# The last head of a decode kernel: an earlier signal for a value buffer, a split load, a new order of chunks and a fifth weight buffer

## Chip, cores, metric

One NeuronCore of a Trainium2 chip. The metric is device time in microseconds from the first to the last instruction as the runs report it; the profile's span is 1.8 us shorter (1923.6 against 1925.44 in the profiled run of the kernel before). Lower is better.

## The reference

One token (Sq = 1) goes through pre-LN attention over a cache and a dense block:

```
D = 640; H, Sk, Dh = 32, 32768, 192; Dff = 1536        # bf16 inputs
q = (layernorm(x) @ wq), split into 32 heads
p = softmax(q . k_cache * Dh**-0.5);   o = p @ v_cache
h  = x + concat(o) @ wo
out = h + relu(layernorm(h) @ w1) @ w2
```

The work is reading: 805 MB of keys and values and 20 MB of weights, each used once.

## The kernel before

Each head's 32768 keys are cut into chunks. For a chunk, VectorE computes the scores of some keys itself (multiply by q, sum), TensorE those of the rest (transposes **T**, then products **S**; ScalarE copies the transposes out of PSUM in between). ScalarE turns scores into weights by exp, into buffers pA (VectorE's keys) and pB (TensorE's). TensorE then sums the values by these weights (**V**). T4, S4, V4 below are those of chunk 4 of the last head; V(30,7) is the sum of chunk 7 of head 30. SyncE issues all large loads, in program order, and waits before each for its place to be free; GpSimd passes most landings on to TensorE (POOLq in the traces). In the code, the label `("PV", h, c)` says that V(h,c) is done, `den_mm` adds up the weights of a head, `o_turn` turns a head's result for the projection. A value tile ("first, second, third values" of the last head) holds two chunks' values; the two places `vt[0]`, `vt[1]` alternate. The last head reads its final quarter in small pieces (the "end keys" and "end values") so that little is left to do after the last byte.

```python
def vals(h, ld):                       # SyncE: one value tile
    if ld == 1 and h > 0:
        g.wait("PV", h, 0)             # V(h,0) done: says that V(h-1,7), before it, has left vt[1]
    elif ld > 1:
        g.wait("PV", h, 2 * ld - 3)
    elif h > 0:
        g.wait("PV", h - 1, 5)
    ...
    load(vt[ld % NV][:], src, f"dv{ld % NV}", "v", h, ld)

# SyncE, last head (LAST = 31):
for ld in range(NL - 1):               # NL = 4
    ...                                # key tile ld
    vals(LAST - 1, NL - 1) if ld == 0 else vals(LAST, ld - 1)   # written as if/else in the kernel
for i, jl in enumerate(ENDJ):          # three end-key loads, no wait of their own
    end_keys(NL - 1 + i, k0, jl, f"dke{1 + i}")
vals(LAST, NL - 2)                     # third values, waits for V1
...                                    # end values (wait for V1), w1 (waits for V3), w2 in three pieces

def pe_end(g):                         # TensorE, last head
    transposes(g, h, 0); den_mm(g, h - 1); scores_pe(g, h, 0)
    for c in range(1, NC - 2):         # c = 1..5
        transposes(g, h, c)
        values(g, *((h - 1, NC - 3 + c) if c < 3 else (h, c - 3)))
        scores_pe(g, h, c)
        if c == 3: o_turn(g, h - 1)
    transposes(g, h, 6); values(g, h, 3)
    for c in (7, 8, 9):
        transposes(g, h, c)
        if c > 7: values(g, h, c - 4)  # V4 before S7, V5 before S8
        scores_pe(g, h, c - 1)
    values(g, h, 6); scores_pe(g, h, 9); values(g, h, 7)
    den_mm(g, h); values(g, h, 8); values(g, h, 9)
    ...                                # projection, norm, both dense layers, output
```

Statements are joined on a line here to save room. The projection of every head pair is added up in PSUM, in the bank `attT`, over the whole run: one starting matmul at the very beginning, all later ones of the projection with `start=False`.

The softmax here doesn't subtract the row's maximum and nothing guards it: scores larger than these inputs give would overflow.

## Time and profile before

| | before |
|---|---|
| median of 3 runs (lowest, highest) | 1924.14 us (1923.79, 1927.06) |
| profiled run, its span | 1925.44, 1923.6 us |
| DMA busy share in 40 slices | 9 tenths or more in 39 |
| HBM read | 825 MB at 429 GB/s |
| TensorE, VectorE busy | 81%, 81% |

TensorE and VectorE are each busy for four fifths of the time and still neither sets it: the transfers do, until the last head. There the order of loads, their landings and TensorE's waits decide. The prediction below shows the lines.

### The profile page before, as it was taken

Reading aid. Unit: us, or ns where it says so; the run is one execution under the profiler, and the core shown is the slowest. Engines: PE = TensorE matmul, PEld = TensorE weight load, DVE = VectorE, ACT = ScalarE, POOL = GpSimd, SP = SyncE. Lnnn points to the kernel's source line nnn. Section 1 sums busy time; section 2 is a strip of 40 time slices with the busy share of each in tenths; the row PEclk is TensorE's granted clock in tenths of the full one; section 3 lists DMA queues with packets and bytes.
Section 4 is the critical chain, followed back from the end, with each engine's and each line's share of the span. In section 5 each row is a group of like instructions: output and inputs, shape, how many; then the busy total and the mean of one; then the engine's idle time right before and its main releaser. Section 6 shows DMA issues by size and latency. Waiting matters only on the chain.

```text
span 1923.6 us, 36300 instructions
## 1 busy us (share of the span) xinstructions
PE 1554.4 (81%) x15899; PEld 1088.3 (57%) x15899; DVE 1560.5 (81%) x734; ACT 966.9 (50%) x2031; POOL 0.7 (0%) x6
## 2 busy tenths in 40 slices
PE   4878878777888788787777878878878788787897
PEld 3555555555555565555555655655656556555564
DVE  5878888878888798787787878978879788888885
ACT  3544545544555454454454545544545445544553
POOL 0000000000000000000000000000000000000000
PEclk8989898887888887888888888888788798898888
DMA  9999999999999999999999999999999999999997
GB/s 408 433 428 434 435 430 440 429 430 435 429 435 437 426 436 432 432 437 429 438 430 429 438 429 433 439 428 433 431 433 435 430 433 436 431 437 432 430 410 328
DMA packets 35864, 825.25 MB, mean 429 GB/s; under 512 B 3588, under 2 KB 5124, under 8 KB 11140
## 3 DMA queue, kind: packets, MB, share of 16 engines
q1 hardware_dynamic: 35834, 824.98, 99.6%
q8 instruction: 12, 0.20, 0.0%
q14 instruction: 8, 0.07, 0.0%
q10 hardware_dynamic: 10, 0.00, 0.0%
HBM read 824.97 MB, written 0.00 MB: 429 GB/s over the span
## 4 chain that ended last, share of the span: by engine, by line
DMA 55%; PE 35%; ACT 6%; DVE 3%; SPq 1%; issue 0%; POOLq 0%; DVEq 0%
DMA kt<-in_A_k_cache_dram 54%; PE o_ps L368 19%; PE tp L387 10%; ACT kT L587 6%; PE sp L368 4%; PE mm L368 2%; DVE pr L672 1%; DVE sc L675 1%; DMA vt<-in_A_v_cache_dram 1%; PE attT L368 1%; SPq L227 1%; ACT pA L602 0%; POOLq L350 0%; DVE o_pair L686 0%; ACT row_e L607 0%
## 5 line engine op out<-in xcount | busy, mean ns | idle before, releaser
L672 DVE TENSOR_TENSOR pr<-kt,qb 128x2304 f32<-128x2304 bf16 (+2 forms) x257 | 755.9, 2941 | 303.9 <-POOLq L321 278.7
L587 ACT COPY kT<-tp 128x1024 bf16<-128x1024 bf16 (+1 forms) x899 | 817.3, 989 | 321.3 <-PE tp L387 320.4
L387 PE MATMUL tp<-ident_f,kt 128*128 128x128 f32 x3459 | 578.1, 334 | 240.8 <-POOLq L350 238.6
L675 DVE TENSOR_REDUCE sc<-pr 128x12 f32<-128x2304 f32 (+2 forms) x257 | 755.3, 2939 | 8.9
L387 PEld LDWEIGHTS tp<-ident_f,kt 128*128 128x128 f32 x3459 | 501.8, 174 | 252.4 <-POOLq L350 244.0
L368 PE MATMUL o_ps<-vt,pB 128*2 128x384 bf16 x2286 | 459.2, 351 | 7.9 <-POOLq L350 7.1
L593 ACT ACTIVATE pB<-sp 128x20 bf16<-128x20 f32 (+2 forms) x258 | 47.8, 185 | 571.5 <-PE sp L368 571.5
L368 PE MATMUL o_ps<-vt,pA 128*2 128x384 bf16 x1778 | 330.6, 326 | 0.0
L368 PEld LDWEIGHTS o_ps<-vt,pB 128*2 128x2 bf16 x2286 | 187.6, 88 | 233.5 <-issue 92.2
L368 PE MATMUL sp<-qm,kT 128*128 128x2 bf16 x6918 | 214.5, 164 | 106.6 <-ACT kT L587 106.3
L368 PEld LDWEIGHTS sp<-qm,kT 128*128 128x128 bf16 x6918 | 192.5, 98 | 187.6 <-ACT kT L587 144.8
L368 PEld LDWEIGHTS o_ps<-vt,pA 128*2 128x2 bf16 x1778 | 150.0, 84 | 142.0 <-issue 3.5
L602 ACT ACTIVATE pA<-sc 128x12 bf16<-128x12 f32 (+2 forms) x257 | 53.4, 208 | 41.4 <-DVEq L65 40.5
L593 ACT ACTIVATION_READ_ACCUMULATOR pB<-sp 128x1 f32 x258 | 50.2, 194 | 0.0
L602 ACT ACTIVATION_READ_ACCUMULATOR pA<-sc 128x1 f32 x257 | 48.7, 190 | 0.0
L686 DVE TENSOR_SCALAR o_pair<-o_ps,rec 2x384 bf16<-2x384 f32 x32 | 19.4, 605 | 6.3 <-PE o_ps L368 1.7
L368 PE MATMUL mm<-wq_s,xn_ln 128*1 (+1 forms) x160 | 18.7, 248 | 3.7 <-POOLq L350 3.7
L680 DVE TENSOR_REDUCE rec<-mm 128x1 f32<-128x20 f32 x32 | 5.7, 179 | 16.3 <-PE mm L368 11.8
L368 PE MATMUL attT<-oT,wo_s 128*128 128x1 bf16 x465 | 16.4, 164 | 0.3 <-DVE oT L696 0.3
L368 PEld LDWEIGHTS mm<-dsums,ones_mat 128*128 128x128 f32 x64 | 15.1, 291 | 0.3 <-issue 0.3
L368 PEld LDWEIGHTS attT<-oT,wo_s 128*128 128x128 bf16 x465 | 14.5, 101 | 0.4 <-DVE oT L696 0.4
L368 PE MATMUL mm<-ones_row,row_e 1*128 1x1 bf16 x384 | 14.0, 159 | 0.0
(71 smaller groups left out, 145.4 us busy)
## 6 DMA issues: line engine op xcount, KB each, us to landing
vt<-in_A_v_cache_dram SPq DMA_DIRECT2D x127, 3072.0 KB, 18.8
kt<-in_A_k_cache_dram SPq DMA_DIRECT2D x62, 6144.0 KB, 32.4
kt<-in_A_k_cache_dram SPq DMA_DIRECT2D x3, 3072.0 KB, 18.3
wq_s<-in_A_wq_dram SPq DMA_DIRECT2D x4, 1920.0 KB, 22.5
wo_s<-in_A_wo_dram SPq DMA_DIRECT2D x16, 480.0 KB, 9.5
kt<-in_A_k_cache_dram SPq DMA_DIRECT2D x1, 1920.0 KB, 15.4
kt<-in_A_v_cache_dram SPq DMA_DIRECT2D x2, 960.0 KB, 22.4
kt<-in_B_w_dram SPq DMA_DIRECT2D x1, 1920.0 KB, 16.7
```

Source lines behind the costliest of these rows:

```text
L227: g.do(lambda: nc.sync.dma_start(out=dst, in_=src), sem, label, by=16)
L368: return lambda: pe.matmul(o, lhsT=w, rhs=r, **kw)
L387: calls.append(lambda b=b, o=o: pe.transpose(out=dst[:, b, :], in_=src[:, o:o + 2 * P].bitcast(f32), identity=ident_f[:]))
L587: g.do(lambda: act.copy(out=kT[c % 2][:, b0:b0 + nb, :], in_=src[:, 0:nb, :].bitcast(bf16)), "act_pe", ("cp", h, c, k))
L593: g.do(lambda: act.activation(out=pB[c % 4][:, 0:jp], in_=sp[:, 0:jp], func=F.Exp, scale=SCALE, accum_out=dsums[:, 2 * c + 1:2 * c + 2]), ...
L602: g.do(lambda: act.activation(out=pA[c % 4][:, 0:jd], in_=sc[c % NC][:, 0:jd], func=F.Exp, scale=SCALE, accum_out=dsums[:, 2 * c:2 * c + 1 ...
L672: g.chain(lambda: dve.tensor_tensor(out=pr[:, 0:j1 - j0, :], in0=src[:, (off + j0) * Dh:(off + j1) * Dh].rearrange("p (j d) -> p j d", d=D ...
L675: g.chain(lambda: dve.reduce_sum(out=sc[c % NC][:, j0:j1], in_=pr[:, 0:j1 - j0, :], axis=X), "dve")
L680: g.chain(lambda: dve.reduce_sum(out=rec[:, 0:1], in_=mm[:, 0:2 * NCM], axis=X), "dve")
L686: g.do(lambda: dve.tensor_scalar_mul(out=o_pair[:, :, 1, :], in0=o_ps[0:2, 0:2 * Dh].rearrange("q (i d) -> q i d", i=2), scalar1=rec[0:2, ...
```

## The change

Intent: let the last head's second values be issued when their place is free and not one sum later; let TensorE start on the third values when half of them are there, and give it other work until then. The diff's core (the lines of pA/pB that only replace 4 by NB, and the new semaphore's name, are cut):

```diff
+    NB = 5                                    # buffers of pA and pB, were 4
@@ SyncE: vals
-            if ld == 1 and h > 0:
+            if ld == 1 and h == LAST:
+                g.wait("vfree")
+            elif ld == 1 and h > 0:
@@ SyncE: third values in two loads
-        vals(LAST, NL - 2)
+        g.wait("PV", LAST, 1)
+        src = rows(v_hd, LAST, P * JL * (NL - 2), JL)
+        n = J * Dh
+        load(vt[0][:, 0:n], src[:, 0:n], "dv0", "v", LAST, NL - 2)
+        load(vt[0][:, n:2 * n], src[:, n:2 * n], "dvh", "vh")
@@ TensorE: values
+        if h == LAST and c == 5:
+            g.wait("vh")
@@ TensorE: pe_end
             transposes(g, h, c)
-            values(g, *((h - 1, NC - 3 + c) if c < 3 else (h, c - 3)))
+            if c == 1:
+                values(g, h - 1, NC - 2)
+            elif c > 2:
+                values(g, h, c - 3)
             scores_pe(g, h, c)
+            if c == 1:
+                values(g, h - 1, NC - 1)
+                pe_group(g, [mmul(attT[0:1, 500:501], ones_row[0:1, 0:1], zero5[0:1, 0:1], start=True, stop=True,
+                                  skip_group_check=True)], ("vfree",))
@@
-        for c in (7, 8, 9):
-            transposes(g, h, c)
-            if c > 7:
-                values(g, h, c - 4)
-            scores_pe(g, h, c - 1)
-        values(g, h, 6)
-        scores_pe(g, h, 9)
-        values(g, h, 7)
+        transposes(g, h, 7)
+        scores_pe(g, h, 6)
+        transposes(g, h, 8)
+        scores_pe(g, h, 7)
+        transposes(g, h, 9)
+        values(g, h, 4)
+        scores_pe(g, h, 8)
+        scores_pe(g, h, 9)
+        for c in (5, 6, 7):
+            values(g, h, c)
```

The tiny matmul exists because the last sum of each of heads 0 to 30 (chunk 7) signals on a semaphore that the engine loops count down, which SyncE's straight-line program can't wait on; the matmul signals on one that it can.

More of the change, by code (lines that the diff above doesn't have):

```diff
@@ L165 @@
     sc = [sbuf(f"sc{i}", [P, J], f32) for i in range(NC)]
-    pA = [sbuf(f"pA{i}", [P, J], bf16) for i in range(4)]
-    pB = [sbuf(f"pB{i}", [P, J], bf16) for i in range(4)]
+    pA = [sbuf(f"pA{i}", [P, J], bf16) for i in range(NB)]
+    pB = [sbuf(f"pB{i}", [P, J], bf16) for i in range(NB)]
     x_row = sbuf("x_row", [DT, P], bf16)
@@ L217 @@
     names += [f"dk{i}" for i in range(NK)] + [f"dv{i}" for i in range(NV)] + ["dwq", "dwo", "dx", "dout"]
-    names += [f"dke{i}" for i in range(4)] + [f"dve{i}" for i in range(4)] + ["dw1"] + [f"dw2_{i}" for i in range(3)]
+    names += [f"dke{i}" for i in range(4)] + ["dvh"] + [f"dve{i}" for i in range(4)] + ["dw1"] + [f"dw2_{i}" for i in range(3)]
     sems = {n: nc.alloc_semaphore(n) for n in names}
@@ L434, in values @@
         src = v_tile(h, ld)
-        a, b = pA[c % 4], pB[c % 4]
+        a, b = pA[c % NB], pB[c % NB]
         calls = []
@@ L592, in exp_pe @@
         g.wait("S", h, c)
-        g.do(lambda: act.activation(out=pB[c % 4][:, 0:jp], in_=sp[:, 0:jp], func=F.Exp, scale=SCALE,
+        g.do(lambda: act.activation(out=pB[c % NB][:, 0:jp], in_=sp[:, 0:jp], func=F.Exp, scale=SCALE,
                                     accum_out=dsums[:, 2 * c + 1:2 * c + 2]), "act_pe", ("ep", h, c))
@@ L601, in exp_dve @@
         g.wait("sc", h, c)
-        g.do(lambda: act.activation(out=pA[c % 4][:, 0:jd], in_=sc[c % NC][:, 0:jd], func=F.Exp, scale=SCALE,
+        g.do(lambda: act.activation(out=pA[c % NB][:, 0:jd], in_=sc[c % NC][:, 0:jd], func=F.Exp, scale=SCALE,
                                     accum_out=dsums[:, 2 * c:2 * c + 1]), "act_pe", ("ed", h, c))
```

## The prediction

> **What bounds the kernel now.** I read the page first, then the chain of waits over the whole run, then everything after 1845 us in finer views, since the diff acts only there (the five-deep p buffers run in every head, but each head's loop body keeps its order).
>
> The page says that transfers bound the run as a whole: slices of the DMA row are nearly all 9, and the chain is mostly key loads.
>
> ```profile
> GB/s 408 433 428 434 435 430 440 429 430 435 429 435 437 426 436 432 432 437 429 438 430 429 438 429 433 439 428 433 431 433 435 430 433 436 431 437 432 430 410 328
> DMA 55%; PE 35%; ACT 6%; DVE 3%; SPq 1%; issue 0%; POOLq 0%; DVEq 0%
> ```
>
> About 430 GB/s in every slice until the last two (410 and 328). So heads 0 to 30 can't gain from this change; what can gain is the last head, from where the queue starves. The two-microsecond windows (columns: stretch, length, busy of PE, PEld, DVE, ACT, POOL; then granted clock, DMA share, GB/s) show where:
>
> ```profile
> 1869.00:1871.00 2.00, 2.00 (x9) 0.88 (x8) 1.98 (x1) 1.08 (x2) 0.00 (x0) 0.65 0.90 377
> 1871.00:1873.00 2.00, 2.00 (x38) 1.32 (x35) 1.98 (x1) 0.14 (x2) 0.00 (x0) 1.00 0.29 123
> 1873.00:1875.00 2.00, 1.29 (x14) 1.22 (x12) 1.74 (x4) 0.68 (x5) 0.00 (x0) 1.00 1.19 344
> ```
>
> One hole. Against 430 GB/s it loses 2 us x (53 + 307 + 86)/430 = **2.07 us** of transfer time. SyncE's own timeline names its cause:
>
> ```profile
> 1848.12 0.43 SPq L227 DMA_DIRECT2D kt<-in_A_k_cache_dram  x1
> 1872.17 0.33 SPq L227 DMA_DIRECT2D vt<-in_A_v_cache_dram  x1
> 1872.54 1.72 SPq L227 DMA_DIRECT2D kt<-in_A_k_cache_dram  x3
> 1878.36 0.33 SPq L227 DMA_DIRECT2D vt<-in_A_v_cache_dram  x1
> ```
>
> Nothing is issued between 1848.12 and 1872.17, when the queue has run dry. The load at 1872.17 is the last head's second values ("v1"). It waits for the first sum of the last head (V0), and the three end-key loads stand behind it. But its place was read last by the two sums before V0, those of head 30's chunks 6 and 7. On TensorE (start, length, what):
>
> ```profile
> 1861.60 1.46 PE L368 MATMUL o_ps<-vt,pB 128*2 128x384 bf16 x8
> 1862.90 1.46 PE L368 MATMUL o_ps<-vt,pA 128*2 128x384 bf16 x8
> ...
> 1868.41 2.75 PE L368 MATMUL o_ps<-vt,pB 128*2 128x384 bf16 x10
> 1871.00 1.14 PE L368 MATMUL o_ps<-vt,pA 128*2 128x384 bf16 x6
> ```
>
> The place is free at 1864.36; V0 ends at 1872.14. So 7.8 us of the wait guards nothing.
>
> The chain of waits over the end then shows what sets the time:
>
> ```profile
> 1848.12 25.57 DMA kt<-in_A_k_cache_dram
> ...
> 1875.63 2.70 PE o_ps L368 x16
> 1878.34 0.02 issue
> 1878.36 19.60 DMA vt<-in_A_v_cache_dram
> ...
> 1898.05 4.26 PE o_ps L368 x16
> ```
>
> The third values ("v2") are issued when V1 ends and land only at 1897.96, behind v1 and the end keys. Then TensorE works without a real pause to the last sum at 1912.84 (14.8 us), and 10.8 us of projection, norm, dense layers and output follow. So two things matter at the end: when v2 lands, and how much TensorE work is left then. TensorE's idle before V2, T6 and V4 is 2.03, 1.99 and 2.53 us, and its granted clock falls to 0.50 at 1899 to 1901 after the last.
>
> **What the Trainium skill says.** "DMA: Bandwidth & Descriptors", section "Queues, rings and completion order": one issuing engine's queue consumes descriptors in ring order on each DMA engine. The trace agrees: v1, end keys and v2 land in issue order at 1882.5, 1887.9 to 1890.7 and 1898.0. So a load issued early still lands in turn, and only the hole is won on the transfer side. "TensorE: Matmul & The Clock Gate", section "What's actually happening": after an idle window of about 3.4 us TensorE runs at half rate. Here 1.19 to 2.53 us of idle already brought 0.5 in the windows, so this trace is harsher; ten sums then took 3.29 us instead of 1.79. "PSUM — Partial Sum Buffer", section "The four PSUM rules": a starting matmul clears the written-bits of its whole bank in its quadrant. The new signalling matmul has start=True in the bank that holds the projection's running sum; that costs no time, but may concern the values. No record of before can show it.
>
> **The change, part by part.** T, S, V are a chunk's transposes, scores, sums. From this timeline at full clock: T of 15 is 1.85, of 12 1.5, of 9 1.15, of 6 0.8 us; S of 30/24/18/12 is 0.85/0.7/0.5/0.4; V of 16/10/8/4 is 2.7/1.95/1.3/0.65.
>
> *Signal.* V(30,7) moves ahead of T2: S1 ends at 1859.83, V(30,7) at 1862.55, one tiny matmul (0.2 us) tells SyncE, v1 is issued near 1862.9 instead of 1872.17. The end keys follow at once. The hole closes: every later transfer lands 2.07 us earlier. Cost: T2 (now 1862.75) has no sums after it, so S2 waits for ScalarE's four copies (3.5 us from 1863.45) until 1867.05, against 1865.55. After it T3 and V0 at low clock as before (about 5.9 us) end at 1873.7; S3, o_turn, T4 start at 1874.8 instead of 1873.78; V1 ends at 1879.4 and v2 is issued 1 us later than before. That is off the path: the queue then holds v1 and end keys until about 1871 + 14.6 = 1885.6 (6.3 MB at 430).
>
> *Landings after.* v1 1880.4; end keys from 1885.9; v2 whole 1895.9, its first half (3.65 us of bytes less) 1892.2; the four end-value pieces 1898.1 to 1903.2; the last dense weights 1915.0 - 2.07 = 1912.9.
>
> *TensorE after T6* (starts at the key landing, 1885.9; S5 is over at 1885.1): T6 1.15, V3 2.7, T7 1.15, S6 0.55, T8 0.8, wait for T7's copies and chunk 6's exp 0.85, S7 0.5, T9 0.8, V4 2.7, S8 0.4, wait for the exp 0.3, S9 0.4, V5 2.7, V6 and V7 3.9, denominator 0.35, V8 and V9 2.05. Sum 21.3 us, end 1907.2. No value load is late: V4 starts at 1894.4 (half landed 1892.2), V5 at 1898.2 (1895.9), V6 at 1900.9 (1898.1), V9 about 1906.5 (1903.2). Here the order pays: S7, S8, S9, T9 no longer stand behind V4's load, and half of v2 is enough for V4.
>
> *Five buffers.* S9 now precedes V5; with four, chunk 9's exp would overwrite chunk 5's weights. Needed for the order, worth nothing itself; 256 bytes per partition.
>
> *Sum.* Last sum 1912.84 to 1907.2: **5.6 us**. Of these 2.07 are the hole, about 1.5 the half-rate V4 (3.29 - 1.79), and the other 2 the waiting at V4 filled with work. The second dense layer starts 4.77 us after the last sum (as 1917.61 after 1912.84), 1911.97; its last ten matmuls need the last weights at about 1913.4, landed 1912.9. Time 1924.14 - 5.6 = **1918.5 us**.
>
> **Rivals.**
> 1. Transfers take over. If the final weights or end-value pieces slip, only the hole counts: 1922.1. For: the last weights have just 0.5 us of slack, and SyncE sits 13.8 us over issuing them. Against: their landing has 4 us of slack today, and moves with the hole.
> 2. The low clock moves with the wait. An idle stretch at T6 or S7 could put T6, V3 or V4 at half rate, 1.5 us or more each: 1920 to 1921. For: T6 and half of V3 ran at 0.53 to 0.62 today, after 1.99 us of idle. Against: that wait shrinks to about 0.8, and 0.71 us before T4 cost nothing.
> 3. The reorder eats it. If S2's wait and the slow T3 grow, V1 and v2's issue slip. It takes 6 us before the queue runs dry again, so I give this little; 1923 to 1925.
>
> **Range and chances.** Best case (early landings, no cold stretch) 1916.5; with rival 2 and part of rival 1, 1921.5. The three runs of before spread over 3.3 us. 2% is 38 us, more than the whole last head's waits, so within 2% is all but certain.
>
> **What would show it.** Right: v1's issue near 1863; no 2 us window under 350 GB/s between 1865 and 1900; v1 landing near 1880; T9 ahead of V4; last sum near 1907; 4.3 us from the second dense layer's end to the span's end, as now. Wrong: a hole elsewhere, a wait over 1 us before V4 to V9, a clock of 0.5 after 1890, dense matmuls waiting for weights, or heads 0 to 30 changed by over 1 us.

## The result

| | before | changed |
|---|---|---|
| median (lowest, highest), runs | 1925.60 us (1923.79, 1927.35), 4 | 1919.86 us (1919.69, 1921.41), 4 |
| span of the profiled run | 1923.6 us | 1918.1 us |
| ratio of fast runs | | 0.9972, 95% interval 0.9955 to 0.9989 |

A ratio is the mean time of one kernel's fast runs over that of the other's of the same rounds, so not quite the ratio of the medians. The gain is 0.28%: clear of the noise. The prediction, 1918.5 us in a range of 1916.5 to 1921.5, held.

**The profile after.** The same two-microsecond windows as in the prediction (stretch, length, busy of TensorE's matmuls (PE), its weight loads (PEld), VectorE (DVE), ScalarE (ACT) and GpSimd (POOL), the granted TensorE clock as a share of full speed, DMA share, GB/s), changed kernel:

```profile
1869.00:1871.00 2.00, 2.00 (x9) 0.93 (x8) 1.97 (x2) 2.00 (x3) 0.00 (x0) 0.50 0.94 401
1871.00:1873.00 2.00, 2.00 (x12) 0.95 (x11) 1.92 (x1) 0.17 (x1) 0.00 (x0) 0.82 1.13 479
1873.00:1875.00 2.00, 1.97 (x38) 1.54 (x37) 0.59 (x4) 0.47 (x4) 0.00 (x0) 1.00 0.94 406
```

The hole (377, 123, 344 GB/s) is gone. SyncE's timeline of the changed kernel says why, and shows the two half loads:

```profile
1862.69 0.33 SPq L228 DMA_DIRECT2D vt<-in_A_v_cache_dram  x1
1863.06 1.38 SPq L228 DMA_DIRECT2D kt<-in_A_k_cache_dram  x3
1879.02 0.81 SPq L228 DMA_DIRECT2D vt<-in_A_v_cache_dram  x2
```

TensorE's timeline before, V4's first part and the second dense layer (start, length, what, and in brackets the idle time and what ended it):

```profile
1898.05 3.29 PE L368 MATMUL o_ps<-vt,pB 128*2 128x384 bf16 x10 [2.53 <-POOLq L350]
...
1917.61 1.71 PE L368 MATMUL attT<-h1T,wq_s 128*128 128x1 bf16 x60 [0.36 <-ACT h1T L649]
```

And that of the changed kernel around V4, then the last sum and the second dense layer:

```profile
1886.20 1.20 PE L395 MATMUL tp<-ident_f,kt 128*128 128x128 f32 x9 [1.06 <-DMA kt<-in_A_k_cache_dram]
...
1893.14 0.60 PE L376 MATMUL sp<-qm,kT 128*128 128x2 bf16 x18 [0.77 <-ACT pB L613]
1893.61 0.85 PE L395 MATMUL tp<-ident_f,kt 128*128 128x128 f32 x6
1894.39 1.79 PE L376 MATMUL o_ps<-vt,pB 128*2 128x384 bf16 x10
...
1905.85 0.81 PE L376 MATMUL o_ps<-kt,pB 128*2 128x384 bf16 x4
...
1911.55 2.18 PE L376 MATMUL attT<-h1T,wq_s 128*128 128x1 bf16 x60 [0.36 <-ACT h1T L669]
```

V4 starts without a wait at 1894.39 (before: 1898.05 after 2.53 us) and its first ten matmuls take 1.79 us, not 3.29. The last sum ends at 1906.66. The chain of waits that ended last no longer runs through the third values, but through the end keys, V3 (whose end lets the first dense weights be issued), SyncE's long issues and the last piece of the second dense weights:

```profile
1863.06 23.10 DMA kt<-in_A_k_cache_dram
...
1887.41 2.70 PE o_ps L376 x16
...
1890.55 4.67 SPq L228
...
1895.26 7.52 SPq L228
...
1902.82 10.43 DMA wq_s<-in_B_w_dram
1913.25 0.05 issue
1913.30 0.44 PE attT L376 x10
```

So the end has changed hands: from TensorE's remaining sums to the last transfer. (Whether SyncE's issues or the rate of the transfers hold it is tested below, with longer runs.)

### The profile page after: what moved, and what is told of

Its sections match the earlier page's. It is cut to its first block, busy times and chain, and to the rows that moved or that the text cites. A ratio compares the mean times of both kernels' runs of the same rounds, so it can differ in the third digit from the quotient of the medians.

```text
span 1918.1 us, 36303 instructions
## 1 busy us (share of the span) xinstructions
PE 1543.9 (80%) x15900; PEld 1078.2 (56%) x15900; DVE 1560.5 (81%) x734; ACT 966.5 (50%) x2031; POOL 0.7 (0%) x6
## 4 chain that ended last, share of the span: by engine, by line
DMA 55%; PE 34%; ACT 6%; DVE 3%; SPq 1%; issue 0%; POOLq 0%; DVEq 0%; ACTq 0%
DMA kt<-in_A_k_cache_dram 54%; PE o_ps L376 18%; PE tp L395 10%; ACT kT L607 6%; PE sp L376 4%; DVE pr L692 2%; DVE sc L695 2%; PE mm L376 1%; SPq L228 1%; PE attT L376 1%; DMA wq_s<-in_B_w_dram 1%; ACT pA L622 0%; ACT row_e L627 0%; POOLq L358 0%; PE mm L596 0%
## 5 line engine op out<-in xcount | busy, mean ns | idle before, releaser
L395 PE MATMUL tp<-ident_f,kt 128*128 128x128 f32 x3459 | 568.0, 330 | 239.6 <-POOLq L358 238.4
L395 PEld LDWEIGHTS tp<-ident_f,kt 128*128 128x128 f32 x3459 | 492.9, 172 | 251.2 <-POOLq L358 243.6
L716 DVE TENSOR_SCALAR oT<-mm,odd 128x3 bf16<-128x3 f32 x32 | 7.1, 223 | 10.2 <-PE mm L376 7.6
## 6 DMA issues: line engine op xcount, KB each, us to landing
wq_s<-in_A_wq_dram SPq DMA_DIRECT2D x4, 1920.0 KB, 23.6
kt<-in_A_k_cache_dram SPq DMA_DIRECT2D x1, 1920.0 KB, 23.1
```

The lines of the kernel that those rows point to most:

```text
L395: calls.append(lambda b=b, o=o: pe.transpose(out=dst[:, b, :], in_=src[:, o:o + 2 * P].bitcast(f32), identity=ident_f[:]))
L716: g.do(lambda: dve.tensor_scalar_mul(out=oT[:], in0=mm[:, 0:3], scalar1=odd[:]), "dve_pe", ("oTc", h))
```

## The experiments

To compare traces whose earlier heads ran a little differently, I count from a **mark**: the first transposes on head 30's second key tile (1820.98 in before, 1820.81 in the changed kernel; the transfers set it). "Row ready" is the start of the last addition (`y_col`). All in microseconds from the mark, from one trace each:

| kernel | second values issued | V4 starts | last sum ends | row ready |
|---|---|---|---|---|
| before, profiled with the result | 51.2 | 77.1 | 91.8 | 98.4 |
| before, second trace | 48.5 | 75.1 | 90.0 | 96.7 |
| signal alone | 39.0 | 74.3 | 89.1 | 95.7 |
| signal alone, told in the old place | 42.2 | 74.6 | 90.2 | 96.9 |
| halves alone | 51.1 | 73.1 | 86.3 | 94.3 |
| halves and order | 50.9 | 74.4 | 86.7 | 94.2 |
| signal and order | 38.8 | 74.7 | 89.5 | 96.1 |
| signal and halves | 40.8 | 71.3 | 84.6 | 92.4 |
| changed (all) | 41.9 | 73.6 | 85.9 | 93.0 |
| minimal | 42.2 | 71.9 | 85.1 | 92.7 |

Timed over five rounds; the first four shared one chip (before: median 1923.79 of 9 runs, 1923.55 to 1925.96), the next four another (before: 1925.56, 1923.54 to 1926.10).

### Signal alone

```diff
 (the changed kernel, with:)
-    NB = 5
+    NB = 4
 third values in one load again; chunks 7 to 9 in the old order
```

> The signal part alone (V(30,7) ahead of T2 and the tiny matmul; third values whole, old order, four buffers). If the hole is what counts, the second values are issued near 1863, transfers land about 1.8 us earlier as in the changed kernel, and the span falls by most of 5.5 us. My theory: only the hole is won. The third values land whole near 1896.2 instead of 1897.96, TensorE waits over 3 us before V4 and does V4 at half clock (over 3.0 us for its first ten matmuls), last sum near 1911.1 (1912.84 before, 1906.5 after), span near 1922, gain 1.5 to 2.5 us, ratio near 0.999.

Measured: 1924.72 us, ratio 1.0001 (0.9988 to 1.0015). The hole is gone (no window under 400 GB/s from 1865 to 1883) and the trace did what was expected: TensorE waits for the whole third values and then does V4 at half clock.

```profile
1895.81 3.29 PE L371 MATMUL o_ps<-vt,pB 128*2 128x384 bf16 x10 [3.74 <-POOLq L353]
```

Last sum at 1910.6, span 1921.4, a gain of 2.2 us by the trace. The timed runs show none. (The traced run, 1923.22 us, was the fastest of its five, and the trace of before that it is compared with took 1925.44.) That contradiction stayed open until the control runs below.

### Halves and order, without the signal

```diff
-            if ld == 1 and h == LAST:
-                g.wait("vfree")
-            elif ld == 1 and h > 0:
+            if ld == 1 and h > 0:
 V(30,7) after T2 again, no signalling matmul; the rest as changed
```

> Order, halves and five buffers without the signal (the first part of the last head as before). The hole must be back (a two-microsecond window under 200 GB/s near 1871 to 1874), end keys land near 1888. My theory: last sum near 1910.5, span near 1921.3, gain 2.3 us. Rival (the early place is all that matters): last sum stays near 1912.8, gain under 0.5 us. Rival (halves carry nearly everything): gain 4 us or more.

Measured: 1920.19 us, ratio 0.9977 (0.9964 to 0.9991); span 1920.0, last sum 1908.2 against 1910.5 expected. The hole is back (389, 147, 307 GB/s). T6 found its keys already landed and ran at full clock: T7 began at 1891.54, against 1893.17 in the trace of before, which is 1.6 of the 2.3 us that I was too slow.

### Halves alone

```diff
 (the kernel before, with:)
-        vals(LAST, NL - 2)
+        g.wait("PV", LAST, 1)
+        src = rows(v_hd, LAST, P * JL * (NL - 2), JL)
+        n = J * Dh
+        load(vt[0][:, 0:n], src[:, 0:n], "dv0", "v", LAST, NL - 2)
+        load(vt[0][:, n:2 * n], src[:, n:2 * n], "dvh", "vh")
 and V5 waits for "vh"
```

> Third values in two halves alone: old order, old wait, four buffers. The hole is there. The first half should land near 1894.3, before T8 is over, so V4 starts near 1895.5 with no wait and at full clock, and everything after it moves up: last sum near 1908.8, then the last dense weights (landing 1915.0 as before) hold the second dense layer: span near 1919.6, gain about 4 us. The theory of the prediction (hole 2.1, half-rate V4 1.5, filled wait 2, the last by the new order) would have halves alone at 2 us or less, because S7, T9, S8 stand behind V4 in the old order.

Measured: 1920.49 us, ratio 0.9980 (0.9966 to 0.9994); span 1919.3 (1919.6 expected). With the hole (356, 258, 233 GB/s), the old order and four buffers, V4 waits 0.25 us and the row is ready 4.1 us earlier than in the before trace that has the hole too. V4 and the last sum (1907.0) came 1.8 us earlier than expected; that the span still fits is because the last weights, as expected, hold the end. The first part of V4 here:

```profile
1893.74 1.79 PE L374 MATMUL o_ps<-vt,pB 128*2 128x384 bf16 x10 [0.25 <-POOLq L356]
```

The second dense layer now waits for its weights, twice:

```profile
1912.18 0.94 PE L374 MATMUL attT<-h1T,wq_s 128*128 128x1 bf16 x30 [0.72 <-DMA wq_s<-in_B_w_dram]
1913.74 1.22 PE L374 MATMUL attT<-h1T,wq_s 128*128 128x1 bf16 x30 [0.63 <-DMA wq_s<-in_B_w_dram]
```

So the split load carries most of the gain, and what remains is set by transfers.

### Signal and halves, old order

> The changed kernel without its new order of the last chunks (old order, four buffers): what the order and the fifth buffer are worth. By the prediction the order fills the wait at V4, so undoing it costs about 2 us: last sum near 1908.5, span 1919.5 to 1920. Rival: with the first half landing near 1892.5, V4 follows T8 at once in the old order too, TensorE has the same work and no 0.8 and 0.4 us waits for exps: last sum near 1906.4, span equal to the changed kernel's within 0.5 us.

Edit: the changed kernel with the loop over `(7, 8, 9)` restored and NB = 4. Measured: 1919.61 us (1919.42 to 1919.68), ratio 0.9975 (0.9961 to 0.9989); span 1917.9. The rival was right: V4 follows T8 almost at once (line below), the last sum ends at 1905.77, and the second dense layer waits 0.54 and 0.63 us for weights.

```profile
1892.50 1.79 PE L376 MATMUL o_ps<-vt,pB 128*2 128x384 bf16 x10 [0.27 <-POOLq L358]
```

Beside the halves the new order gained nothing; by these traces it costs TensorE about 1.3 us at the last sum (85.9 against 84.6), of which the waiting weights swallow half. The signal, beside the halves, is worth about 1 us: halves alone took 1920.49 us in the same rounds (1919.68 to 1921.93), also with a wider spread.

### Signal and order, third values whole

Edit: the changed kernel with `vals(LAST, NL - 2)` in one load.

> The changed kernel with its third values in one load again: what the halves are worth beside signal and order. All times are counted from the mark, the first transposes on head 30's second key tile (near 1821 us). The output row is ready (y_col) at 98.4 us from it in the kernel before, 92.9 in the changed one, 95.7 with the signal alone, 94.3 with the halves alone, 92.4 with both and the old order. If the halves are what frees TensorE, V4 must wait about 1.8 us for the whole load here (after T9, which the order now puts first), last sum 87.5 from the mark (85.7 in the changed kernel), y_col 94 to 95. Rival (order does the halves' work): V4 waits under 0.5 us and y_col is at 93 or less.

Measured: 1921.91 us, ratio 0.9983 (0.9969 to 0.9996). V4 waits 1.79 us for the whole load, as expected, and all of it then ran at half clock:

```profile
1895.66 3.36 PE L371 MATMUL o_ps<-vt,pB 128*2 128x384 bf16 x10 [1.79 <-POOLq L353]
1898.81 2.13 PE L371 MATMUL o_ps<-vt,pA 128*2 128x384 bf16 x6
```

From V4's start to the next product that is 5.2 us, against 2.7 in the changed kernel, so the last sum came at 89.5 where I expected 87.5. Order does not do the halves' work. But it is not worthless where the load is whole: V4 waits 1.79 us here and 3.74 with the old order (signal alone, both versions), and the median is 1921.91 us against 1923.67 for the next experiment in the same rounds (which also leaves the sum in its old place). So order and halves fill the same wait; with the halves none is left for the order.

### Signal alone, told in the old place

```diff
             values(g, *((h - 1, NC - 3 + c) if c < 3 else (h, c - 3)))
+            if c == 2:
+                pe_group(... the tiny matmul, start=False ..., ("vfree",))
```

> Signal alone, but told where the last sum of head 30 stood before (after T2), so no sum is moved ahead of T2. Settles two things: whether the signal alone is worth 2 to 3 us (as the trace of the first version says) or nothing (as its timed runs said, interval -2.3 to +2.9 us), and whether moving the sum matters. Expected: issue of the second values near 1864.5, no hole, S2 about 1.5 us earlier, same landings as in the first version, V4 waiting 3 us or more for the whole third values; last sum 89 and y_col 95.7 from the mark, time 1.5 to 3 us under before. If moving the sum cost something, y_col comes at 94.5 or less.

Measured: 1923.67 us, ratio 0.9992 (0.9979 to 1.0006): the interval includes none. No hole, second values issued at 1863.52, V4 again after 3.74 us and at half clock. Moving the sum ahead of T2 isn't needed. But as in the first version, a trace without a hole, and no clear gain; the row came at 96.9 from the mark where I expected 95.7. In this trace T3 and V0 ran at full clock and V0 was over by 1868.8, so even a load that waits for V0 would have been issued in time: this trace doesn't show that the signal closed anything.

### Two controls: the kernel before, without a hole

The first control was meant for another question (below): the kernel before with one constant changed.

> Control for the values: the kernel before, with the projection's running sum (attT) seeded with 1.0 instead of 0.0 at the start and 1.0 subtracted when it is read. Nothing may clear it in between. Expected: correct.

It came out correct, at 1923.26 us, and its trace has no hole. So I took the kernel before once more:

> A second trace of the kernel before, unchanged. The seeded control, whose program is the kernel before but for one constant, issued its second values at 1869.2 instead of 1872.2 and had no hole, at 1923.26 us; the first trace of before had the hole, at 1925.44 us. If the hole is there in some runs only, this run's time goes with its trace: under 1924 us with the second values issued before 1870.5 and no two-microsecond window under 350 GB/s from 1865 to 1880, or over 1924.5 us with a later issue and a hole of 1.4 to 2.3 us. Rival (the hole is always there and the spread is something else): a hole at under 1924 us, or none at over 1924.5 us.

Measured: 1923.50 us, no window under 389 GB/s from 1865 to 1880. TensorE's T3 and V0 in that run, and SyncE's issue of the second values:

```profile
1865.02 1.51 PE L387 MATMUL tp<-ident_f,kt 128*128 128x128 f32 x12
1866.46 1.79 PE L368 MATMUL o_ps<-vt,pB 128*2 128x384 bf16 x10
1868.09 1.14 PE L368 MATMUL o_ps<-vt,pA 128*2 128x384 bf16 x6
```

```profile
1869.26 0.33 SPq L227 DMA_DIRECT2D vt<-in_A_v_cache_dram  x1
```

In the first trace of before, T3 and the first part of V0 took 2.17 and 2.75 us, and the issue came at 1872.17. In all five traces of kernels that wait for V0, the hole goes with T3 and V0 at low clock: before (issue 1872.2, hole), halves and order (1872.4, hole), halves alone (1871.8, hole), against the two controls (1869.2, 1869.3, none). The low clock is not the first link. S2, just before T3, had waited 1.19 to 1.36 us for ScalarE's copies in the three traces with the hole, and not at all in the controls. The first trace of before, then the second:

```profile
1865.55 0.90 PE L368 MATMUL sp<-qm,kT 128*128 128x2 bf16 x30 [1.19 <-ACT kT L587]
1866.32 2.17 PE L387 MATMUL tp<-ident_f,kt 128*128 128x128 f32 x12
```

```profile
1864.26 0.90 PE L368 MATMUL sp<-qm,kT 128*128 128x2 bf16 x30
```

ScalarE makes these copies after its exp of VectorE's scores of chunk 1, and those ended at 1861.3 to 1861.9 in the traces with the hole, at 1859.0 and 1860.2 in the controls. So of the 2.9 us between the two issues about 1.3 are S2's lateness and 1.6 the low clock after it; why VectorE was later in some runs was not followed further back.

So the hole belongs to some runs of before, not to all, and by these traces the signal alone buys only what such a run lost. This would explain both results of the signal alone: on the first chip five of before's nine runs were under 1924 us, on the second one of nine. (Another run of before beside the second trace took 1925.36 us.) That every slow run of before has a hole is not shown; V4's half-clock stretch, which varied from 2.6 to 3.4 us for its first ten matmuls in these traces, moves the time too.

### The least that does it

Edit: the kernel before with the tiny matmul after V(30,7) in its old place, with `start=False`, the wait on it, and the two half loads. Old order, four buffers.

> The least of the change: signal told in the old place (by a matmul that does not start a new accumulation), third values in halves, old order, four buffers. If order, moved sum and fifth buffer are worth nothing, it equals signal plus halves: y_col 92.4 from the mark, median near 1919.6, the last dense weights holding the second dense layer. Rival (the moved sum is needed, because the second values are now issued 1.9 us later): hole or late end keys, y_col 93.5 or later.

Measured: 1919.69 us (1919.52 to 1920.05), ratio 0.9971 (0.9957 to 0.9984), row ready at 92.7. Equal to the changed kernel, with a smaller spread. T4 waited for keys and ran cold here (3.46 us), V1 ended only at 1881.3 and the half loads were issued 2.4 us later than in the changed kernel, which cost nothing: the queue still had bytes.

### Longer runs for the last weights

```diff
-            load(w2_s[:, c0:c1], B_w2.rearrange("(c p) n -> p c n", p=P)[:, c0:c1], ...)
+            load(w2_s[:, c0:c1], B_w2.rearrange("(p c) n -> p c n", p=P)[:, c0:c1], ...)
-        pe_group(g, [mmul(o_ps[:, f:f + 1], w1_s[:, c, f * P:(f + 1) * P], hn[:, c:c + 1],
+        pe_group(g, [mmul(o_ps[:, f:f + 1], w1_s[:, c, f:Dff:FT], hn[:, c:c + 1],
```

> The minimal kernel with the second dense weights laid out so that each partition reads one run of 2560 to 7680 bytes instead of 1280-byte rows (h1's order follows by a strided weight load). Tests whether the end is now set by the transfers' rate in their last microseconds (395 to 416 GB/s there against 430), and by SyncE's 15 us over issuing them. Expected: SyncE issues the three in under 2 us, the rate stays above 420 GB/s, the last weights land 0.4 to 0.7 us earlier, y_col near 91.8 from the mark, median 0.3 to 0.8 us under the minimal kernel's: too little for the timed runs alone. If SyncE's long issue itself held them up, more than 1 us.

Measured: 1920.38 us, ratio 0.9977 (0.9963 to 0.9990), slower than the minimal kernel. The transfer side did what was hoped: 424 to 426 GB/s at 1905 to 1909 where the minimal kernel has 393 to 402, SyncE's three issues in 8.4 us instead of 14.5 (under 2 us expected: wrong), the last weights landed 0.4 us earlier (91.7 from the mark against 92.1), and no wait for weights. So SyncE's issue and the transfers' rate together cost the minimal kernel about 0.4 us at that landing. But the weights of the first dense layer are now read with a step of 12 elements, and that doubled the layer. The first dense layer's instructions (duration min/median/max in ns), this kernel and then the minimal one:

```profile
L376 PEld LDWEIGHTS o_ps<-xn_ln,kt x60: 141/167/168, 1908.5 to 1911.9; 128*128 128x128 bf16 x60
```

```profile
L376 PEld LDWEIGHTS o_ps<-xn_ln,kt x60: 95/96/99, 1908.9 to 1910.4; 128*128 128x128 bf16 x60
```

The layer took 3.64 us against 1.65. Low clock is not the reason: in the changed kernel, where the windows show 0.56 for this layer, the loads with step 1 took 104 ns and the layer 1.76 us. The Trainium skill has a reason ("SBUF — State Buffer", section "Door 1: The DMA port swizzle (why `[64,N]` ≈ `[32,N]`)"): SBUF is read in lines of 16 bytes, and bf16 strides are free only up to 8 elements. A step of 12 leaves the line at every element; the measurement agrees, but no other step was tried, and I had not looked it up.

### Does the signalling matmul touch the running sum?

The prediction noted that a starting matmul clears the written-bits of its bank, and that the change puts one into the bank of the projection's sum. The outputs passed the comparison all the same. By an estimate from the reference's inputs they would in any case: values of scale 0.05 averaged over 32768 keys are near 0.0003, and through `wo` (0.05 times 6144 to the power -0.5, 6144 terms) about 0.00001, beside an x of scale 0.05. So I made the sum visible: seed it with 1.0 at the start, subtract 1.0 when it is read.

```diff
-        pe_group(g, [mmul(attT[:, 0:DT], ident_b[:], zero5[:], start=True, ...
+        pe_group(g, [mmul(attT[:, 0:DT], ident_b[:], one5[:], start=True, ...      # one5 holds 1.0
-        ... out=h_col[:], in0=attT[:, 0:DT], scalar=1.0, in1=x_col[:], op0=A.mult, ...
+        ... out=h_col[:], in0=attT[:, 0:DT], scalar=1.0, in1=x_col[:], op0=A.subtract, ...
```

The kernel before with it is the first control above: correct. The changed kernel with it:

> The changed kernel with the same seed. Its signalling matmul has start=True and writes partition 0 of the bank that holds the running sum. If it clears the written-bits of that bank in its 32 partitions, the next projection overwrites there, the seed (and all earlier heads' sums) is lost on 32 of 128 partitions, and 160 of 640 outputs are wrong by about 1: WRONG. If only its own element is touched: correct.

Measured: WRONG, relative error 1.14 (single run, 1919.23 us). And with `start=False` in the signalling matmul:

> As the last, with start=False in the signalling matmul alone. Expected: correct, whichever way the last goes; if the last is wrong and this is right, the flag is the cause.

Measured: correct (single run, 1919.89 us). So the change as given loses part of the sum, and the flag is the cause. That it is exactly heads 0 to 29 on 32 of the 128 partitions is what the rule of the page that the prediction cites says ("PSUM — Partial Sum Buffer", section "The four PSUM rules"); the runs show only that the seed is lost somewhere and that the flag decides. The minimal kernel has `start=False` and costs no time for it.

## Why the prediction was right, point by point

**The number.** The span was to fall by 5.6 us and fell by 5.5 (1923.6 to 1918.1). The time came out 1.4 us above the prediction for a reason outside the kernel: I took the trace's difference off the median (1924.14), while the traced run itself took 1925.44. 1925.44 - 5.6 = 1919.8; measured 1919.86. The difference of two traces belongs to the traced run's time. There is luck in it: against the second trace of before (span 1921.7) the span fell by only 3.6 us.

**The hole: right in this trace, wrong as a property of the kernel.** It closed, and the end keys landed 1.8 us earlier (1886.2 against 1887.9; 2.07 expected), the last weights 1.75. But other runs of before have none. The second values landed at about 1881.6 instead of 1880.4, and V2 waited 0.51 us. The prediction had moved their old landing by the size of the hole; why they came later is not shown.

**V4 without its wait and at full clock: right to the tenth** (1894.39, predicted 1894.4; 1.79 us). **Its cause: wrong.** I gave the 2 us of filled waiting to the new order. Halves alone, in the old order, started V4 at 73.1 from the mark; all parts together at 73.6. The half load did it; the order only moved S7 and T9 in front, and with S7 a wait for an exp (0.77 us; S9 waits for another, 0.36 us, after V4). The order does fill such a wait where the load is whole, but then V4 ran at half clock. I should have walked the old order with the halves through the same sum; that takes five minutes and gives 1892.3 (1892.50 in the trace of signal and halves).

**TensorE after T6**: 21.3 us predicted, 20.5 measured. **The last weights' slack of 0.5 us: wrong.** They landed at 1913.25, not 1912.9, and the last ten matmuls had to wait for them; my first rival came half true, for 0.2 us in the changed kernel, and for 0.5 to 1.4 us in four others (halves alone, halves and order, signal and halves, minimal). The two errors cancelled: the row was ready at 1913.76, and the prediction's steps give 1913.7.

**Five buffers**: needed for the new order only. A build of the changed kernel with four failed the race check before the chip (a write to pB1 while a sum still reads it), and the old order with four is as fast.

**Clock.** My second rival, low clock at T6 to V4, did not happen; a wait of 1.06 us before T6 cost nothing. It happened where nobody waits for it, at T3 and V0 (0.50 at 1869 to 1871). The second dense layer ran at 0.50 too, but that its matmuls took 2.18 us instead of 1.71 is mostly the wait for the last weights: at 0.50 without such a wait they took 1.76 (second trace of before).

## What to carry to other kernels

When a sum waits for a load that sits in a full queue, splitting that load costs a few lines and lets the work start half a load earlier; try it before reordering anything. A gain that one trace shows in a wait of a few microseconds may belong to that run: trace the old kernel twice before building on it. And a "harmless" signalling matmul has side effects in its PSUM bank; test the values with a seed that is large enough to be seen.

## What the Trainium skill lacked or had wrong

- "TensorE: Matmul & The Clock Gate" ("What's actually happening") has half rate after an idle window of about 3.4 us, and says that the window is free-running. It has no figure for single idles far shorter than a window. Here 1.19 us of idle before S2 was followed by 0.50 (T3 at 2.17 us instead of 1.51) and 1.79 us before V4 by a whole V4 at half rate, while 1.06 us before T6 and 2.03 us before V2 (in before) cost nothing. So by these runs the length of a short idle does not say whether the clock falls. Two traces of one kernel that differ in this, among other things, differ by 1.9 us in span.
- No page that I found has how long SyncE itself is held by loads of many short runs while earlier loads are still queued: 13.8 to 15.8 us for 1.97 MB in 1280-byte runs, 8.4 us in runs of 2560 to 7680 bytes.
- "SBUF — State Buffer" gives the stride limit but no duration: 167 ns for a 128x128 bf16 weight load at a step of 12 elements, 96 ns at step 1.
